# Turned attention probabilities: three PSUM banks of a unit become two, and three small transpositions become one

## The chip, the cores and the metric

The kernel runs on one core of a Trainium2 chip. The metric is the device time of one execution in microseconds (us). Five engines work side by side, each through its own list of instructions in order: PE (matrix multiplications and transpositions; its weight loads are listed as PEld), DVE (vector work), ACT (activations and copies), POOL (more vector work), SP (here it only issues DMAs). PE writes its results to PSUM, which has eight banks of 128 partitions by 512 fp32 columns; DVE and ACT read them from there.

## What is computed

Three stages follow one another: attention with a window of 128 keys and four sink keys that every query sees, then a feed-forward stage with a cosine (FFN), then a mixture of eight experts, one for each token.

```python
# B, H, S, D = 4, 8, 768, 64
keep = is_sink | in_window
scores = np.where(keep, scale * q @ k.T, -1e9)
a = np.exp(scores - scores.max(-1))
a = a / (a.sum(-1) + 1e-9)
x = (a @ v)                       # to 3072 tokens x 512
h = x @ w_in                      # 512 -> 2048
x = (h * np.cos(h)) @ w_out       # 2048 -> 512
# top-1 experts: out[e] = gate * (relu(x @ w1[e]) @ w2[e])
```

## The kernel before

The sequence of each batch is cut into two halves of 384 queries, which gives eight half-batches, hb = 0 to 7, and each half-batch into three blocks of 128 queries (t = 0, 1, 2). The eight heads are taken in four pairs (pr = 0 to 3). One pair of one half-batch is a unit; there are 32. The FFN of a half-batch runs while the units of the next half-batches run: `attn_half` and `run_ffn` are generators that hand back weights, and `merge` interleaves them by these weights, so that PE always has FFN products (tiles `hp`, L136, and `y`, L640) between the small steps of a unit. From what the generators emit, a list scheduler makes the final order of each engine's list. After it, an engine takes its instructions strictly in that order.

The change lies in `rest()` of `attn_front`, the last part of a unit. There the unnormalised probabilities `Pb` (128 queries by 272 columns: 128 older keys, 16 sinks, 128 own keys) are scaled by 1/sum (by POOL for hb = 2, by DVE from hb = 3). For a block t that is *folded*, the older and the own 128 columns were added into one square, since every query has a window over exactly one of the two at each column. Then, for each t: PE turns (transposes) the two heads' squares into a PSUM tile `pt` (L560), and DVE reads `pt` into `pT`, each square twice, once with each of two triangular masks `sides` (L148 is the helper that records it). A block that is not folded takes four transpositions or two (L569, L570) and a copy by ACT (L572). Then the 16 sink columns of both heads are copied into `pc` (L589), PE turns them, for each t by itself, into another PSUM tile `pz` (L592: 32 rows each), ACT copies `pz` to `sp` (L593), and PE multiplies `sp` and `pT` with the values, into `po`.

Units differ as follows. In hb = 0 and 1 nothing is folded. In hb = 3, 5, 7 all three blocks are, and the sinks of all three go through `pz` (12 units). In hb = 2, 4, 6 only t = 2 is folded and has sinks to be turned (12 units); t = 0 and t = 1 go through ACT. PSUM tiles of the attention part (`pq`, `pk`, `ps`, `pt`, `pz`, `po`) come from `psb`, which takes one of three banks in rotation.

Of the kernel before, what the change touches and what calls it, by code (L numbers as in the profile page):

```python
# [11 lines left out]
F32 = DT.float32  # L12
# [4 lines left out]
AF = mybir.ActivationFunctionType  # L17
# [3 lines left out]
P = 128  # L21
# [33 lines left out]
NPOOL = 3  # L55
# [6 lines left out]
def kernel(  # L62
# [23 lines left out]
    HALF = S // 2  # L86
# [227 lines left out]
    def steps(hb):  # L314
        return STEPS_0 if hb <= 1 else STEPS_1
# [80 lines left out]
    def attn_front(hb, pr):  # L396
# [138 lines left out]
        def rest():  # L535
# [16 lines left out]
            pT = apool.tile([P, 2, NQ * 256], F32, name="pT", bufs=2)  # L552
            for t in range(NQ):
                pt = psb("pt").rearrange("p (j x) -> p j x", j=2)
                first = half == 0 and t == 0
                s0 = P if first else 0
                if folded(t):
                    pt2 = pt[:, 0]
                    for j in range(2):
                        PE.transpose(pt2[:, j * P:(j + 1) * P], Pb[t][j][:, SEG:W3], ident)  # L560
                    s4 = [P, 2, 2, P]
                    tt(DVE, pT[:, :, t * 256:(t + 1) * 256].rearrange("p j (x q) -> p j x q", x=2),
                       pt2.rearrange("p (j q) -> p j q", j=2).unsqueeze(2).to_broadcast(s4),
                       sides.unsqueeze(1).to_broadcast(s4), ALU.mult)
                    yield steps(hb)[4]
                    continue
                for j in range(2):
                    if not first:
                        PE.transpose(pt[:, j, 0:P], Pb[t][j][:, 0:P], ident)  # L569
                    PE.transpose(pt[:, j, P:2 * P], Pb[t][j][:, SEG:W3], ident)  # L570
# [11 lines left out]
            t0 = 2 if half == 0 else 0  # L582
            pc = apool.tile([P, NQ, 2, NS], F32, name="pc")
            if extra:
                for t in range(t0, NQ):
                    for j in range(2):
                        POOL.tensor_copy(pc[:, t, j], Pb[t][j][:, P:SEG])
            else:
                (POOL if hb < NPOOL else DVE).tensor_copy(pc[:, t0:], Pt[:, t0:, :, P:SEG])  # L589
            pz = psb("pz")  # L590
            for t in range(t0, NQ):
                PE.transpose(pz[0:2 * NS, t * P:(t + 1) * P], pc[:, t].rearrange("p j s -> p (j s)"), ident)  # L592
            ACT.activation(out=sp[0:2 * NS, t0 * P:], in_=pz[0:2 * NS, t0 * P:HALF], func=AF.Copy)  # L593
            yield steps(hb)[5]
# [808 lines left out]
```

## Time and profile before

| | us |
|---|---|
| median of three runs | 1149.26 (1148.4 to 1151.08) |
| the profiled execution | 1149.4 |
| its span in the trace | 1147.6 |
| PE busy | 1093.7 |
| DVE / ACT busy | 716.4 / 629.4 |

The trace covers one execution; 1.8 us of its time lie around the span. In the order of time: up to 126 us the first eight units and the conversion of weights, from 126 to 690 us the 24 units of hb = 2 to 7 woven into the FFN, to 812 us the rest of the FFN, to 1090 us the experts, then the tail. The page says how long each engine was busy. A timeline row gives start, duration, engine, line, what is written from what, and in brackets how long the engine had been idle before, and which instruction released it. PE's durations overlap, since products are pipelined: the price of a PE instruction in a full stream is the distance from its start to the next start.

### The profile page before, as it was taken

Reading aid. Unit: us, or ns where it says so; the run is one execution under the profiler, and the core shown is the slowest. Engines: PE = TensorE matmul, PEld = TensorE weight load, DVE = VectorE, ACT = ScalarE, POOL = GpSimd, SP = SyncE. Lnnn points to the kernel's source line nnn. Section 1 sums busy time; section 2 is a strip of 40 time slices with the busy share of each in tenths; the row PEclk is TensorE's granted clock in tenths of the full one; section 3 lists DMA queues with packets and bytes.
Section 4 is the critical chain, followed back from the end, with each engine's and each line's share of the span. In section 5 each row is a group of like instructions: output and inputs, shape, how many; then the busy total and the mean of one; then the engine's idle time right before and its main releaser. Section 6 shows DMA issues by size and latency. Waiting matters only on the chain.

```text
span 1147.6 us, 20806 instructions
## 1 busy us (share of the span) xinstructions
PE 1093.7 (95%) x6504; PEld 936.0 (82%) x6504; DVE 716.4 (62%) x2206; ACT 629.4 (55%) x1283; POOL 224.8 (20%) x275
## 2 busy tenths in 40 slices
PE   5989999999999999999999999999999998999995
PEld 3667677888888888878888889899889997899994
DVE  6678888877876877886788774746741225622210
ACT  4878887766676676666777553434222225522221
POOL 1232224211111111111111112321112211121110
PEclk9999999999999999999999999999999999999998
DMA  6566666433333433433253223723151115111110
GB/s 149 139 193 197 195 200 168 113 86 84 95 91 83 118 82 75 112 86 83 72 118 96 69 78 107 251 62 111 47 193 53 61 39 184 33 62 41 39 42 24
DMA packets 139286, 118.56 MB, mean 103 GB/s; under 512 B 96367, under 2 KB 105583, under 8 KB 139120
## 3 DMA queue, kind: packets, MB, share of 16 engines
q1 hardware_dynamic: 134800, 103.02, 32.3%
q0 software_dynamic: 4320, 13.65, 3.6%
q8 instruction: 65, 1.06, 0.4%
q14 instruction: 101, 0.83, 0.2%
HBM read 151.06 MB, written 19.67 MB: 149 GB/s over the span
## 4 chain that ended last, share of the span: by engine, by line
PE 76%; DVE 12%; ACT 4%; DMA 4%; issue 2%; POOL 1%; SPq 0%; DVEq 0%; POOLq 0%; ACTq 0%
PE hp L136 19%; PE y L640 18%; PE m_y L136 10%; PE m_h L136 10%; PE po L136 5%; PE ps L136 4%; DMA out_dram<-m_ot,m_ids 3%; PE pl L768 1%; DVE pT L148 1%; DVE qT L148 1%; DVE ch L142 1%; DVE kl L148 1%; PE m_a L1107 1%; PE pq L445 1%; PE pt L570 1%
## 5 line engine op out<-in xcount | busy, mean ns | idle before, releaser
L148 POOL TENSOR_TENSOR g_l<-ch,g_h 128x384 fp32r<-128x384 f32 x128 | 133.4, 1043 | 552.9 <-ACT g_h L712 497.6
L136 PE MATMUL hp<-xT_h,wi_h 128*128 128x384 f32 x512 | 182.2, 356 | 2.7 <-DVE ch L148 2.7
L136 PE MATMUL hp<-xT_l,wi_h 128*128 128x384 f32 x512 | 174.7, 341 | 0.0
L136 PE MATMUL hp<-xT_h,wi_l 128*128 128x384 f32 x512 | 174.1, 340 | 0.0
L640 PE MATMUL y<-wo,g_h 128*128 128x512 f32 x384 | 157.2, 411 | 0.0
L640 PE MATMUL y<-wo_l,g_h 128*128 128x512 f32 x384 | 156.0, 406 | 0.0
L640 PE MATMUL y<-wo,g_l 128*128 128x512 f32 x384 | 154.6, 403 | 0.2 <-POOL g_l L148 0.2
L702 ACT ACTIVATE ch<-ch,cols 128x384 f32<-128x384 f32 x128 | 78.9, 617 | 119.4 <-DVE ch L145 117.6
L136 PE MATMUL m_y<-wi_h,hT 128*128 128x512 f32 x416 | 132.5, 393 | 0.7 <-ACT m_ot L1149 0.5
L145 DVE SCALAR_TENSOR_TENSOR hT<-m_h,hT 128x256 fp32r<-128x256 f32 x88 | 37.4, 425 | 151.9 <-ACTq L1301 94.9
L136 PEld LDWEIGHTS hp<-xT_h,wi_h 128*128 128x128 f32 x512 | 96.8, 189 | 10.7 <-issue 3.4
L136 PEld LDWEIGHTS hp<-xT_l,wi_h 128*128 128x128 f32 x512 | 96.9, 189 | 5.5 <-issue 1.9
L142 DVE TENSOR_SCALAR ch<-hp 128x384 int32<-128x384 f32 x128 | 71.0, 555 | 48.0 <-PE hp L136 36.2
L136 PEld LDWEIGHTS hp<-xT_h,wi_l 128*128 128x128 f32 x512 | 96.5, 189 | 1.2 <-issue 0.9
L712 ACT ACTIVATE g_h<-ch 128x384 fp32r<-128x384 f32 x128 | 66.5, 521 | 54.1 <-DVE ch L148 42.9
L148 DVE TENSOR_TENSOR ch<-ch,hp 128x384 f32<-128x384 f32 x128 | 70.4, 550 | 38.3 <-ACT ch L702 37.9
L136 PEld LDWEIGHTS m_y<-wi_h,hT 128*128 128x128 f32 x416 | 78.0, 188 | 16.9 <-issue 0.9
L532 ACT ACTIVATE Pb<-Pb,mx 128x272 f32<-128x272 f32 (+1 forms) x168 | 83.0, 496 | 9.3 <-DVE mx L516 8.4
L640 PEld LDWEIGHTS y<-wo,g_l 128*128 128x128 f32 x384 | 72.3, 188 | 14.2 <-POOL g_l L148 0.8
L1118 ACT ACTIVATE hT<-m_h 128x256 fp32r<-128x256 f32 x88 | 34.0, 387 | 88.0 <-PE m_h L136 80.9
L136 PE MATMUL m_y<-wi_l,hT 128*128 128x512 f32 x208 | 81.0, 389 | 0.0
L640 PEld LDWEIGHTS y<-wo,g_h 128*128 128x128 f32 x384 | 72.4, 189 | 10.5 <-issue 2.7
(280 smaller groups left out, 2368.1 us busy)
## 6 DMA issues: line engine op xcount, KB each, us to landing
rw<-in_moe_w_dram SPq DMA_DIRECT2D x112, 512.0 KB
wo_l<-wl_scr SPq DMA_DIRECT2D x122, 256.0 KB
cv_in<-in_moe_w_in_dram SPq DMA_DIRECT2D x16, 512.0 KB
cv_out<-in_moe_w_out_dram SPq DMA_DIRECT2D x16, 512.0 KB
y_scr<-yt SPq DMA_DIRECT2D x24, 256.5 KB
xT_h<-xg_h SPq DMA_DIRECT2D x32, 192.0 KB
xT_l<-xg_l SPq DMA_DIRECT2D x32, 192.0 KB
qn<-in_q_dram SPq DMA_DIRECT2D x56, 96.0 KB
```

The source lines that it names most:

```text
L136: PE.matmul(o, l, r, start=start, stop=stop)
L142: e.tensor_scalar(out=o, in0=i, scalar1=s1, scalar2=s2, op0=op0, op1=op1)
L145: e.scalar_tensor_tensor(out=o, in0=i0, scalar=s, in1=i1, op0=op0, op1=op1)
L148: e.tensor_tensor(out=o, in0=a, in1=b, op=op)
L445: PE.transpose(pq[:, t * P:(t + 1) * P], qn[:, t].rearrange("p j d -> p (j d)"), ident)
L532: ACT.activation(out=Pb[t][j][:, c0:c1], in_=Pb[t][j][:, c0:c1], func=AF.Exp, scale=-1.0, bias=mx[:, i:i + 1], accum_out=sm[:, i:i + 1])
L570: PE.transpose(pt[:, j, P:2 * P], Pb[t][j][:, SEG:W3], ident)
L640: i = PE.matmul(o, l, r, start=start, stop=stop)
L702: ACT.activation(out=ch, in_=ch, func=AF.Sin, scale=TWO_PI, bias=half_pi)
L712: ACT.activation(out=gh, in_=ch, func=AF.Copy)
L768: return PE.matmul(pl[0][:, 0:NE], yT[:, c, :], wg[:, c, :], start=c == 0, stop=c == KD - 1)
L1118: ACT.activation(out=hT_h[f], in_=hp, func=AF.Relu)
```

## The change

For hb = 2 to 7 (`whole`) the copy into `pc` is written ahead of the transpositions of the probabilities. The blocks t = 0 and t = 1, where folded, share one PSUM bank (columns 0 to 255 and 256 to 511). Block t = 2 takes the first half of another bank, and the sinks are turned into columns 256 to 383 of that bank, directly behind the two transpositions of t = 2, with one transposition for all blocks (96 rows for hb = 3, 5, 7; 32 rows, as before, for hb = 2, 4, 6). ACT's copy to `sp` then comes block by block: three of 32x128 in place of one of 32x384, each from another group of 32 partitions. It is written behind DVE's reading of the same bank, and both weights that the generator hands back now come together behind it. Units of hb = 0 and 1 keep their code.

```diff
--- before.py
+++ after.py
@@ -550,20 +550,38 @@
                         ts(DVE, Pb[t][j][:, c0:c1], Pb[t][j][:, c0:c1], sm[:, i:i + 1], ALU.mult)
             yield steps(hb)[3]
             pT = apool.tile([P, 2, NQ * 256], F32, name="pT", bufs=2)
+            t0 = 2 if half == 0 else 0
+            pc = apool.tile([P, NQ, 2, NS], F32, name="pc")
+            if whole:
+                (POOL if hb < NPOOL else DVE).tensor_copy(pc[:, t0:], Pt[:, t0:, :, P:SEG])
+            bank = None
             for t in range(NQ):
-                pt = psb("pt").rearrange("p (j x) -> p j x", j=2)
                 first = half == 0 and t == 0
                 s0 = P if first else 0
                 if folded(t):
-                    pt2 = pt[:, 0]
+                    if t == 2 or bank is None:
+                        bank = psb("pt")
+                        pt2 = bank[:, 0:2 * P]
+                    else:
+                        pt2 = bank[:, 2 * P:4 * P]
                     for j in range(2):
                         PE.transpose(pt2[:, j * P:(j + 1) * P], Pb[t][j][:, SEG:W3], ident)
+                    if t == NQ - 1:
+                        pz = bank[:, 2 * P:3 * P]
+                        nz = 2 * NS * (NQ - t0)
+                        PE.transpose(pz[0:nz], pc[:, t0:].rearrange("p t j s -> p (t j s)"), ident)
                     s4 = [P, 2, 2, P]
                     tt(DVE, pT[:, :, t * 256:(t + 1) * 256].rearrange("p j (x q) -> p j x q", x=2),
                        pt2.rearrange("p (j q) -> p j q", j=2).unsqueeze(2).to_broadcast(s4),
                        sides.unsqueeze(1).to_broadcast(s4), ALU.mult)
+                    if t == NQ - 1:
+                        for t_ in range(t0, NQ):
+                            z0 = 2 * NS * (t_ - t0)
+                            ACT.activation(out=sp[0:2 * NS, t_ * P:(t_ + 1) * P], in_=pz[z0:z0 + 2 * NS], func=AF.Copy)
+                        yield steps(hb)[5]
                     yield steps(hb)[4]
                     continue
+                pt = psb("pt").rearrange("p (j x) -> p j x", j=2)
                 for j in range(2):
                     if not first:
                         PE.transpose(pt[:, j, 0:P], Pb[t][j][:, 0:P], ident)
@@ -579,19 +597,19 @@
                 for t in range(NQ):
                     POOL.tensor_copy(rb[t].rearrange("p (j d) -> p j d", d=D),
                                      sm[:, 2 * t:2 * t + 2].unsqueeze(2).to_broadcast([P, 2, D]))
-            t0 = 2 if half == 0 else 0
-            pc = apool.tile([P, NQ, 2, NS], F32, name="pc")
-            if extra:
+            if not whole:
+                if extra:
+                    for t in range(t0, NQ):
+                        for j in range(2):
+                            POOL.tensor_copy(pc[:, t, j], Pb[t][j][:, P:SEG])
+                else:
+                    POOL.tensor_copy(pc[:, t0:], Pt[:, t0:, :, P:SEG])
+                pz = psb("pz")
                 for t in range(t0, NQ):
-                    for j in range(2):
-                        POOL.tensor_copy(pc[:, t, j], Pb[t][j][:, P:SEG])
-            else:
-                (POOL if hb < NPOOL else DVE).tensor_copy(pc[:, t0:], Pt[:, t0:, :, P:SEG])
-            pz = psb("pz")
-            for t in range(t0, NQ):
-                PE.transpose(pz[0:2 * NS, t * P:(t + 1) * P], pc[:, t].rearrange("p j s -> p (j s)"), ident)
-            ACT.activation(out=sp[0:2 * NS, t0 * P:], in_=pz[0:2 * NS, t0 * P:HALF], func=AF.Copy)
-            yield steps(hb)[5]
+                    PE.transpose(pz[0:2 * NS, t * P:(t + 1) * P], pc[:, t].rearrange("p j s -> p (j s)"), ident)
+                ACT.activation(out=sp[0:2 * NS, t0 * P:], in_=pz[0:2 * NS, t0 * P:HALF], func=AF.Copy)
+                yield steps(hb)[5]
+
             def band(blk):
 
                 own = blk if half == 0 else blk - 1
```

Three places show the order that the scheduler makes of it. The first is PE's list in unit hb = 3, pr = 1, from directly behind the transpositions of t = 2 past those of the sinks. `y` and `hp` are FFN products. Before:

```order
L640 MATMUL y_3139<-wo_l,g_h 128x512
L640 MATMUL y_3139<-wo_114,g_l 128x512
L640 MATMUL y_3140<-wo_114,g_h 128x512
L640 MATMUL y_3140<-wo_l,g_h 128x512
L640 MATMUL y_3140<-wo_114,g_l 128x512
L136 MATMUL hp<-xT_h,wi_h_85 128x384
L136 MATMUL hp<-xT_l,wi_h_85 128x384
L136 MATMUL hp<-xT_h,wi_l_95 128x384
L592 MATMUL pz<-ident,pc 32x128 x3
L136 MATMUL hp<-xT_h,wi_h_85 128x384
L136 MATMUL hp<-xT_l,wi_h_85 128x384
L136 MATMUL hp<-xT_h,wi_l_95 128x384
```

After, from directly behind the transpositions of t = 2 up to the first `po`:

```order
L658 MATMUL y_3132<-wo_l,g_h 128x512
L658 MATMUL y_3132<-wo_114,g_l 128x512
L572 MATMUL pt<-ident,pc 96x128
L658 MATMUL y_3133<-wo_114,g_h 128x512
L658 MATMUL y_3133<-wo_l,g_h 128x512
L658 MATMUL y_3133<-wo_114,g_l 128x512
L658 MATMUL y_3134<-wo_114,g_h 128x512
L658 MATMUL y_3134<-wo_l,g_h 128x512
L658 MATMUL y_3134<-wo_114,g_l 128x512
L136 MATMUL hp<-xT_h,wi_h_85 128x384
L136 MATMUL hp<-xT_l,wi_h_85 128x384
L136 MATMUL po<-sp_139,vs_n_137 64x384 x2
```

The turned sinks stood three `hp` and five `y` behind t = 2's transpositions, and stand two `y` behind them now; where three instructions were, there is one of 96 rows. `po`, which stood six `hp` behind the sinks, now stands six `y` and two `hp` behind them.

In the same unit, DVE's list (`kl`, `qT` belong to the next unit's keys and queries, `ch` to the FFN). Before:

```order
L148 TENSOR_TENSOR qT<-pq,qT 64x384
L148 TENSOR_TENSOR kl_2754<-pk,kT 64x4x128
L148 TENSOR_TENSOR pT<-pt,sides 128x2x256 x2
L142 TENSOR_SCALAR ch<-hp 128x384
L589 COPY pc<-Pb_3209 128x96
L145 SCALAR_TENSOR_TENSOR ch<-hp,ch 128x384
```

After:

```order
L148 TENSOR_TENSOR qT<-pq,qT 64x384
L148 TENSOR_TENSOR kl_2751<-pk,kT 64x4x128
L556 COPY pc<-Pb_3203 128x96
L148 TENSOR_TENSOR pT<-pt,sides 128x2x256 x2
L142 TENSOR_SCALAR ch<-hp 128x384
L145 SCALAR_TENSOR_TENSOR ch<-hp,ch 128x384
```

The copy into `pc` moved from behind the two `pT` readings and a step of the FFN to ahead of both, directly behind `kl`.

The last unit of hb = 3 (pr = 3), PE's list from the FFN products ahead of the sinks to the first `po` (`ps`: scores of the next unit). Before:

```order
L640 MATMUL y_3138<-wo_l,g_h 128x512
L640 MATMUL y_3138<-wo_123,g_l 128x512
L640 MATMUL y_3139<-wo_123,g_h 128x512
L640 MATMUL y_3139<-wo_l,g_h 128x512
L592 MATMUL pz<-ident,pc 32x128 x3
L640 MATMUL y_3139<-wo_123,g_l 128x512
L640 MATMUL y_3140<-wo_123,g_h 128x512
L640 MATMUL y_3140<-wo_l,g_h 128x512
L640 MATMUL y_3140<-wo_123,g_l 128x512
L136 MATMUL ps<-kT,qT 128x128
L136 MATMUL po<-sp_139,vs_n_137 64x384 x2
```

After:

```order
L136 MATMUL hp<-xT_l,wi_h_1765 128x384
L572 MATMUL pt<-ident,pc 96x128
L136 MATMUL hp<-xT_h,wi_l_1771 128x384
L136 MATMUL hp<-xT_h,wi_h_1765 128x384
L136 MATMUL hp<-xT_l,wi_h_1765 128x384
L568 MATMUL pt<-ident,Pb_3736 128x128 x2
L136 MATMUL hp<-xT_h,wi_l_1771 128x384
L136 MATMUL hp<-xT_h,wi_h_1765 128x384
L136 MATMUL hp<-xT_l,wi_h_1765 128x384
L136 MATMUL hp<-xT_h,wi_l_1771 128x384
L658 MATMUL y_3132<-wo_123,g_h 128x512
L136 MATMUL po<-sp_139,vs_n_137 64x384 x2
```

The sinks stand ahead of two transpositions of t = 1 now, which wait for the reading of t = 0 in the same bank; the rest of `y` moved behind `po`.

## Rows read from the trace of the kernel before

**Rows 1.** The page: busy us of each engine (x instructions), and its chain of waits.

```profile
...
PE 1093.7 (95%) x6504; PEld 936.0 (82%) x6504; DVE 716.4 (62%) x2206; ACT 629.4 (55%) x1283; POOL 224.8 (20%) x275
...
PE 76%; DVE 12%; ACT 4%; DMA 4%; issue 2%; POOL 1%; SPq 0%; DVEq 0%; POOLq 0%; ACTq 0%
...
```

**Rows 2.** Busy time of each engine in the window from 126 to 690 us.

```profile
...
126.00:690.00 564.00, 549.02 (x3245) 464.96 (x3245) 444.01 (x1395) 390.64 (x765) 111.15 (x125) 1.00 0.40 103
...
```

**Rows 3.** Instructions on tile pz, 126 to 690 us: min/median/max ns; then waits (us, times).

```profile
...
L592 PE MATMUL pz<-ident,pc x48: 269/272/283, 131.1 to 683.3; 128*32 128x128 f32 x48
L593 ACT ACTIVATE sp<-pz x24: 248/374/485, 131.9 to 683.6; 32x128 f32<-32x128 f32 x12, 32x384 f32<-32x384 f32 x12
...
  DVE pc L589: 1.7, 3
...
  PEld po L136: 4.6, 15
...
```

**Rows 4.** Instructions on tile pt, the same window, columns as in Rows 3.

```profile
...
L148 DVE TENSOR_TENSOR pT<-pt,sides x48: 665/684/694, 130.6 to 682.2; 128x512 f32<-128x512 f32 x48
...
```

**Rows 5.** Timeline, PE, one unit: start us, us, instruction [idle before <-releaser].

```profile
...
248.84 0.41 PE L560 MATMUL pt<-ident,Pb 128*128 128x128 f32 x2 [0.47 <-DVE pT L148]
...
251.08 0.38 PE L560 MATMUL pt<-ident,Pb 128*128 128x128 f32 x2
...
251.53 0.40 PE L640 MATMUL y<-wo,g_l 128*128 128x512 f32 x1
...
251.76 0.40 PE L640 MATMUL y<-wo,g_h 128*128 128x512 f32 x1
...
252.63 0.34 PE L136 MATMUL hp<-xT_l,wi_h 128*128 128x384 f32 x1
...
252.80 0.34 PE L136 MATMUL hp<-xT_h,wi_l 128*128 128x384 f32 x1
...
252.98 0.49 PE L592 MATMUL pz<-ident,pc 128*32 128x128 f32 x3
...
253.48 0.34 PE L136 MATMUL hp<-xT_l,wi_h 128*128 128x384 f32 x1
...
254.47 0.87 PE L136 MATMUL po<-sp,vs_n 128*64 128x384 f32 x4
...
```

**Rows 6.** Timeline of the same unit, DVE and ACT.

```profile
...
250.18 0.69 DVE L148 TENSOR_TENSOR kl<-pk,kT 64x512 fp32r<-64x512 f32 x1
...
250.91 1.29 DVE L148 TENSOR_TENSOR pT<-pt,sides 128x512 f32<-128x512 f32 x2
...
252.57 0.20 DVE L589 COPY pc<-Pb 128x96 f32<-128x96 f32 x1
...
253.29 0.62 ACT L702 ACTIVATE ch<-ch,cols 128x384 f32<-128x384 f32 x1 [3.09 <-DVE ch L145]
...
253.93 0.48 ACT L593 ACTIVATE sp<-pz 32x384 f32<-32x384 f32 x1
...
```

**Rows 7.** Timeline of a second unit, PE and DVE, DVE late.

```profile
...
298.14 0.41 PE L560 MATMUL pt<-ident,Pb 128*128 128x128 f32 x2 [0.41 <-DVE qT L148]
...
302.09 1.89 DVE L148 TENSOR_TENSOR pT<-pt,sides 128x512 f32<-128x512 f32 x3
...
304.36 0.20 DVE L589 COPY pc<-Pb 128x96 f32<-128x96 f32 x1
...
304.71 0.49 PE L592 MATMUL pz<-ident,pc 128*32 128x128 f32 x3 [0.61 <-DVE pc L589]
...
306.25 0.87 PE L136 MATMUL po<-sp,vs_n 128*64 128x384 f32 x4
...
```

**Rows 8.** Timeline of a third unit, DVE and PE.

```profile
...
343.39 0.69 DVE L759 COPY yT<-yT 128x512 f32<-128x512 f32 x1
...
344.57 0.56 DVE L148 TENSOR_TENSOR kl<-pk,kT 64x384 fp32r<-64x384 f32 x1
...
344.93 0.38 PE L560 MATMUL pt<-ident,Pb 128*128 128x128 f32 x2
...
```

## The prediction

> **What bounds the kernel now.** I read the page first: PE is busy 95% of the span and holds 76% of the chain of waits, DVE 12% [rows 1]. An average hides stages, so next the window in which all changed units lie, 126 to 690 us: PE is busy 549.02 of 564.00 us, DVE 444 and ACT 391 [rows 2]. PE is the bound there too, and only 15 us of idle time are left in it. So time comes from there in two ways alone: PE does less, or PE waits less. A step of another engine counts by the wait that it makes on PE. Then the views of the two tiles: the sinks' transpositions, their copy, and who waits for them [rows 3], and the reading of the turned probabilities [rows 4]. At last I went through the timeline of units, to see what PE does between the steps and what DVE and ACT do meanwhile [rows 5 to 8].
>
> **What the change removes.** In 12 units three sink transpositions become one: of the 48 in the window [rows 3] 24 remain. The 269 to 283 ns of such a row overlap their neighbours, so the price is the distance between starts. From the `hp` product at 252.80 to the one at 253.48 there are three transpositions and one further product; two product steps of 0.17 (252.63 to 252.80) are 0.34, and 0.34 of the 0.68 remain for three, 0.113 each [rows 5]. Nothing in the trace has 96 rows: if such a one costs as much as three of 32, nothing is saved, if as one, 24 are. I take one: t = 2's pair of 128 rows at 251.08 and one `y` of 0.23 take 0.45 up to the `y` at 251.53, so 0.11 each [rows 5], the same as those of 32. So PE loses 24 x 0.113 = 2.7 us of work. That is 0.23 in each of the 12 units. It is certain as work, and all of it lies on PE.
>
> **What it adds on ACT.** For 12 units one copy of 32x384, 485 ns, becomes three of 32x128, 248 ns each [rows 3]: 0.74 in place of 0.48, 0.26 more, or 3 us over all 12. ACT has 173 us idle in the window [rows 2], so this costs nothing by itself; it counts where `po` waits for the last copy.
>
> **What it makes wait.** The sinks had a bank of their own. Now the built order has three links in a row that were apart: the sinks' transposition waits for `pc`; DVE's reading of t = 2 waits for that transposition; ACT's first copy waits for DVE's reading, though it reads other columns of the bank. One reading is 0.68 us [rows 4]. Behind a waiting transposition stands all of PE's list, FFN products included; behind the waiting copies stands ACT's FFN work. The Trainium skill, "PSUM — Partial Sum Buffer", section "PSUM bank collisions raise a hardware error", says that two engines must not touch the same bank in the same quadrant of partitions at once, reads with reads included, so that software must order them. By it the third link is needed wherever banks are shared, and speaks against this change: without it the copy would start 0.68 earlier than I reckon below. The trace of before has no such pair, so no row shows it.
>
> Three units show what the links cost.
>
> *First unit* (hb = 3, pr = 1) [rows 5, 6]. The second block's transpositions start at 248.84 in both orders, held by the reading of the first. From there PE has six `hp` (to 250.14), one `y`, t = 2's two (t = 2 was held by nothing that is longer now), and two `y` of 0.23 (251.53 to 251.76), and comes to the sinks at 251.05. DVE ends `kl` at 250.87 and then copies `pc`, 0.20, to 251.07; with 0.15 from a copy's end to the transposition's start (304.56 to 304.71 in [rows 7]) that gives 251.25: a wait of 0.2 that was not there, since before `pc` had ended at 252.77 for a transposition at 252.98. Then one transposition, six `y`, two `hp`: `po` is reached at about 253.1. DVE reads both blocks from 251.07 to 252.43; three copies take ACT to 253.2 (it was idle until 253.29), and `po` starts at about 253.25, with a wait of 0.15. Before, `po` waited 0.1 for the copy that ended at 254.41. New waits 0.2 + 0.15 - 0.1 = 0.25, saved 0.23: nothing gained. The other units of this kind vary around it, by my reckoning from 0.05 to 0.25 of new waits, as `kl` ends a little earlier or later. I take 0.2 for ten units (nine with pr = 0 to 2, and the last unit of hb = 7, in another order): +2.0.
>
> *Second unit* (hb = 3, pr = 3; hb = 5 has the same order) [rows 7]. DVE is late: it comes to the readings at 302.09 only. Before, PE waited at the sinks to 304.71, where the last product before them allowed about 303.92: 0.8 (the row books 0.61 of it). Now `pc` goes first, to 302.29, and PE is at the sinks at 301.3 (from 298.14: two transpositions, nine `y`, five `hp`), so it waits 1.15, to 302.44. Then, with three `hp`, two transpositions, four `hp` and one `y`, `po` is reached at 304.2, where the readings (to 304.33) and three copies (303.7 to 304.45) let it start at 304.5: 0.3. That is 1.45 for 0.8: +0.65 in each of two units, +1.3.
>
> *Third unit* (hb = 4, pr = 1; hb = 6 likewise) [rows 8]. Here the number of transpositions stays, but the order moves: five `y` come between the first block and the second instead of three, so the second now comes to DVE's `yT` copy, which ends at 344.08, and the third to `kl`, which ends at 345.13 (before it started at 344.93). Each waits 0.15: +0.3, twice +0.6.
>
> *The other ten units* (four of hb = 2, whose `pc` POOL makes, and three each of hb = 4 and 6) keep one sink transposition and lose no work; their new waits lie behind other waits or FFN products as far as I can follow them: 0, with -0.2 and +0.3 for each from the units above as bounds, hence -2 to +3.
>
> **Sum.** -2.7 + 2.0 + 1.3 + 0.6 = +1.2 us. Part of any shift, up or down, is given back: PE's next wait for DVE, ACT or a DMA absorbs it, and 15 us of such waits are there [rows 2]; I take half of it away, +0.6. The profiled execution took 1149.4 (1147.6 of it span), 0.14 above the median of 1149.26. 1149.4 + 0.6 = 1150.0. About 0.2%, 2.3 us, is what a measurement of this kernel can tell from no change: this is none, 1147.0 to 1151.6.
>
> **Rivals.** *The waits do not come about.* If `kl` and `pc` end some tenths earlier, as they may when DVE's list shifts with PE, the sinks find `pc` ready and `po` finds the copies done. For it: the waits in the first unit are 0.2 and 0.15 on a reckoning of events some 4 us long. Besides, the three waits of PE for `pc`, 1.7 us, and the waits of `po` for the copy, 4.6 us in 15 cases [rows 3], are there to be lost. Then all of the 2.7 is kept and about half of the 1.7: 1149.4 - 2.7 - 0.8 = 1145.9. Against it: DVE reaches `pc` behind `kl` in every unit I followed. Chance 0.24 for a gain over 0.2%, mostly between 1145 and 1147.
>
> *The chain gets longer and `po` waits for it: slower.* Place: from `pc` through the transposition, the reading and the copies to `po`. Price: in the first unit it leaves `po` about 0.15 late; each further 0.1 us by which DVE is late goes into PE's wait one for one. If DVE is half a microsecond later than I reckon in each of the 12 units with three copies (the second unit shows that it can be over one), that is 6.0 on top of the +1.2; with half absorbed as above, +3.6: 1153.0. This decides from about 0.3 us in each: 12 x 0.3 + 1.2 = 4.8, half of it 2.4. For it: DVE is 79% busy in the window. Against it: half the sites have FFN products to spare. Chance 0.30.
>
> *It does not do what it says.* The shared bank is meant to free one in the rotation. But the second block waits for the reading of the first already before [rows 5], so the two had one bank by the rotation; nothing new comes free at once. This is in the forecast and gives its number.
>
> **How the numbers follow.** Forecast (no difference that can be told) 0.46, faster 0.24, slower 0.30. The range leaves out the ends of both: 1146.3 to 1153.8. Faster means under 1147.0, slower over 1151.6.
>
> **What would show it.** Right: PE instructions fewer by 24; 24 rows of sink transpositions in it in place of 48; a new wait of PE on `pc` in units of hb = 3 and 5, some 3 us in all against 1.7; ACT's copies start when a reading ends; the window's PE busy time lower by 2 to 3 us with its length within 2. Wrong, fast side: PE's idle time in the window stays at 15 us or falls, and the 2.7 appears whole. Wrong, slow side: PE's waits for `pc` and `sp` in this window together are over 10 us, against 6.3 (1.7 + 4.6).

## The result, and the profile after

The change makes the kernel slower: 1158.45 us (1157.57 to 1159.33) against 1149.98 (1148.4 to 1151.08), a ratio of 1.0072 with a 95% interval of 1.0057 to 1.0087. Measured once more beside other kernels it was 1158.11 against 1151.42, 1.0054 (1.0035 to 1.0074). The forecast was 1150.0 and no difference, with a range up to 1153.8.

The page of the changed kernel, its busy times and its chain of waits, which answer to [rows 1]:

```profile
PE 1098.0 (95%) x6480; PEld 938.4 (81%) x6480; DVE 719.9 (62%) x2206; ACT 631.9 (55%) x1307; POOL 224.6 (19%) x275
...
PE 73%; DVE 14%; DMA 4%; ACT 4%; issue 2%; POOL 1%; SPq 0%; ACTq 0%; DVEq 0%; POOLq 0%
```

PE issues the 24 instructions fewer that were foreseen (6480 for 6504), yet its busy time rose by 4.3 us, and in the chain PE's share fell from 76 to 73% while DVE's rose from 12 to 14%. A record of PE is drawn out where the granted clock is lower: a `y` product takes 0.63 us in a stretch at 0.50 that is shown below, 0.40 in [rows 5]. So a busy time that rises need not mean more work. The stretch of [rows 2], six us longer now:

```profile
126.00:696.00 570.00, 551.14 (x3221) 465.13 (x3220) 447.65 (x1396) 393.88 (x791) 112.19 (x125) 0.99 0.39 102
```

PE has 18.9 us without a record in it, against 15 before, and its granted clock (the third number from the end) is 0.99 in place of 1.00. PE's busy time in it is 2.1 us higher, where the prediction had 2 to 3 us less.

To see where the time went I laid the two traces on one another by the transpositions of the queries (`pq`), one group for each unit, and by the first transposition of the experts (`m_a`). The last part of a unit, where the change lies, runs behind the `pq` of the unit that follows it. The rows in the kernel before (start, duration, instruction), where the first eight units are done, where those of hb = 2 are done, and at the experts:

```profile
123.26 0.49 PE L445 MATMUL pq<-ident,qn 128*128 128x128 f32 x3
...
218.65 0.49 PE L445 MATMUL pq<-ident,qn 128*128 128x128 f32 x3
...
841.01 1.03 PE L1107 MATMUL m_a<-ident,m_yg 128*128 128x128 f32 x8
```

The same three in the changed kernel:

```profile
123.82 0.49 PE L445 MATMUL pq<-ident,qn 128*128 128x128 f32 x3
...
222.73 0.49 PE L445 MATMUL pq<-ident,qn 128*128 128x128 f32 x3
...
847.86 1.03 PE L1125 MATMUL m_a<-ident,m_yg 128*128 128x128 f32 x8
```

They are 0.56, 4.08 and 6.85 us late. Read as differences of such starts for every unit, the time was lost like this (a unit's step is the growth of the lateness over its last part; the second measurement's trace is beside it):

| lost in, us | hb = 2 | hb = 3 | hb = 4 | hb = 5 | hb = 6 | hb = 7 to the experts | sum |
|---|---|---|---|---|---|---|---|
| changed kernel | 3.51 | 0.56 | 0.51 | 0.58 | 0.52 | 0.60 | 6.28 |
| the same, second trace | 3.11 | 0.59 | 0.53 | 0.58 | 0.51 | 0.63 | 5.95 |

From hb = 3 on the two traces agree within 0.05 us per half-batch. Of the 9.2 us between the two spans (1156.8 and 1147.6), 0.56 lie ahead of this stretch and 2.35 behind the start of the experts, where the code is the same; these were not followed up, and no part of what follows rests on them. Two traces of one and the same kernel differ there too, by up to 2 us ahead and 0.8 behind. In the tables below "sum" is always the stretch from the end of the first eight units to the experts.

### The profile page after: what moved, and what is told of

It is laid out like the page before. It is cut to its first block, busy times and chain, and to the rows that moved or that the text cites. A ratio compares the mean times of both kernels' runs of the same rounds, so it can differ in the third digit from the quotient of the medians.

```text
span 1156.8 us, 20792 instructions
## 1 busy us (share of the span) xinstructions
PE 1098.0 (95%) x6480; PEld 938.4 (81%) x6480; DVE 719.9 (62%) x2206; ACT 631.9 (55%) x1307; POOL 224.6 (19%) x275
## 4 chain that ended last, share of the span: by engine, by line
PE 73%; DVE 14%; DMA 4%; ACT 4%; issue 2%; POOL 1%; SPq 0%; ACTq 0%; DVEq 0%; POOLq 0%
PE hp L136 18%; PE y L658 17%; PE m_h L136 10%; PE m_y L136 10%; PE po L136 5%; PE ps L136 5%; DMA out_dram<-m_ot,m_ids 3%; DVE pT L148 2%; DVE qT L148 2%; DVE kl L148 2%; PE pl L786 1%; DMA cv_in<-in_moe_w_in_dram 1%; PE pt L588 1%; PE pq L445 1%; PE m_a L1125 1%
```

## Where the waits are

The copies to `sp` in the changed kernel, their min/median/max and waits, which answer to [rows 3]:

```profile
L580 ACT ACTIVATE sp<-pt x48: 249/267/269, 132.0 to 690.5; 32x128 f32<-32x128 f32 x48
...
  DVE pT L148: 32.2, 17
...
  PEld po L136: 7.4, 16
```

Before, `po`'s weight load waited 4.6 us for the copy; now 7.4, and ACT stands idle for 32.2 us in all ahead of the copies until DVE has read, where before it stood 12.0 us until the sinks were turned. Idle time of ACT is no loss by itself; `po`'s wait is. The first unit of the prediction (hb = 3, pr = 1), PE, DVE, POOL and ACT, which answers to [rows 5, 6]:

```profile
253.04 0.41 PE L568 MATMUL pt<-ident,Pb 128*128 128x128 f32 x2 [0.45 <-DVE pT L148]
...
254.39 0.69 DVE L148 TENSOR_TENSOR kl<-pk,kT 64x512 fp32r<-64x512 f32 x1
...
254.48 1.00 POOL L148 TENSOR_TENSOR g_l<-ch,g_h 128x384 fp32r<-128x384 f32 x1 [4.70 <-ACT g_h L730]
...
255.11 0.44 DVE L556 COPY pc<-Pb 128x96 f32<-128x96 f32 x1
255.59 1.29 DVE L148 TENSOR_TENSOR pT<-pt,sides 128x512 f32<-128x512 f32 x2
...
255.61 0.31 PE L572 MATMUL pt<-ident,pc 128*96 128x128 f32 x1 [0.18 <-DVE pc L556]
...
256.91 0.83 ACT L580 ACTIVATE sp<-pt 32x128 f32<-32x128 f32 x3 [2.50 <-DVE pT L148]
...
257.32 0.33 PE L136 MATMUL hp<-xT_l,wi_h 128*128 128x384 f32 x1
...
257.79 0.87 PE L136 MATMUL po<-sp,vs_n 128*64 128x384 f32 x4
```

The links are the ones foreseen, in their order: `kl` ends at 255.08, `pc` follows, PE stands at the sinks from about 255.27 to 255.61, DVE reads both blocks from 255.59, three copies run from 256.91, and `po`, which could start at 257.49, starts at 257.79. But the copy into `pc` takes 0.44 us, not the 0.20 of [rows 6]: it starts while POOL's `g_l` runs (254.48 to 255.48) and ends 0.07 us behind it, where before POOL was idle.

Half-batch 2 holds more than half of the loss. The place where most of it arises, POOL, DVE and PE in its third unit, after:

```profile
175.39 0.22 DVE L539 RECIPROCAL sm<-sm 128x2 f32<-128x2 f32 x2
...
175.57 1.29 POOL L148 TENSOR_TENSOR g_l<-ch,g_h 128x384 fp32r<-128x384 f32 x1 [4.66 <-ACT g_h L730]
...
176.84 2.81 POOL L142 TENSOR_SCALAR Pb<-Pb,sm 128x128 f32<-128x128 f32 x6
...
177.70 0.68 PE L588 MATMUL pt<-ident,Pb 128*128 128x128 f32 x2 [1.72 <-POOL Pb L142]
```

And before:

```profile
172.35 0.22 DVE L539 RECIPROCAL sm<-sm 128x2 f32<-128x2 f32 x2
...
172.60 3.31 POOL L142 TENSOR_SCALAR Pb<-Pb,sm 128x128 f32<-128x128 f32 x6 [4.89 <-DVE sm L539]
...
173.63 0.38 PE L570 MATMUL pt<-ident,Pb 128*128 128x128 f32 x2
```

DVE comes to the reciprocal of the sums (L539) at 175.39, behind four conversions of weights (`cv_a`, `wo_l`) and a step of the FFN that stood behind it before; it was there at 172.35, and only 0.6 of this is lateness that the unit had from its start (171.46 for 170.88). In POOL's list `g_l` went ahead of the scaling as well. POOL therefore scales the probabilities from 176.84 on, not from 172.60, and PE, whose next transposition needs them, waits 1.72 us. The unit's order of work is another one, though hb = 2 saves no transposition.

## Experiments

### In which half-batches the time is lost

Theory A: the loss sits in hb = 2, whose lists the scheduler ordered anew; the links of the shared bank cost a little elsewhere. Rival B: the links cost alike in all 24 units. Three kernels (e1 to e3) take the changed code for some half-batches and keep the code of before for the others (first branch: the changed code, second: that of before; "hb > 2" in the first kernel, "hb == 2" in the second, "half == 1" in the third):

```diff
+            if not whole or hb > 2:
+                ...
+            else:
+                ...
```

e1, from hb = 3 on: 

> Half-batch 2 keeps the code of before; the changed code runs from hb = 3 on. Theory A (half-batch 2 lost most: its lists were ordered anew, PE waited 1.2 and 1.7 us there and ran at a granted clock of 0.62 to 0.85 afterwards, +3.9 us by the alignment of the two traces at 218.65 and 222.73, less what stood before): about 1152 to 1154, and the granted clock is 1.00 from 126 to 224 us. Rival B (the links between pc, the transposition, the reading and the copies cost in every unit alike, 8.5 us over 24): 1157, since 20 of the 24 units keep them.

e2, hb = 2 alone: 

> The changed code in half-batch 2 alone, before elsewhere; no transposition is saved there. Theory A: 1150 + 3.9 = about 1154, with the granted clock under 1.00 between 140 and 182 us. Rival B: 4 of 24 units, 1.4 us: about 1151.4.

e3, hb = 3, 5, 7 alone: 

> The changed code for hb = 3, 5, 7 alone, where 24 transpositions go; 2, 4 and 6 as before. Theory A, with the sum of the prediction for these 12 units (-2.7 + 2.0 + 1.3): within 1 us of before, 1149 to 1151.5. Rival B: half of 8.5, 1154. If the links cost nothing: 1147.3.

e5, the changed kernel once more: 

> The changed kernel as it is, beside the others. The change in half-batch 2 alone cost 3.2 us at the medians and the change from hb = 3 on cost 0.3, which adds up to 1.003 of before, not to 1.0072. If the two add up: 1154 to 1155. If they work on each other (the bank rotation of every later unit shifts with the banks that hb = 2 takes): 1157 to 1159 again, with steps of 0.15, 0.3 and 0.05 us in the units of hb = 4 and 6, which are missing where hb = 2 keeps its code.

| changed code in | ratio (95%) | hb = 2 | hb = 3 | hb = 4 | hb = 5 | hb = 6 | sum, us |
|---|---|---|---|---|---|---|---|
| all | 1.0054 (1.0035 to 1.0074) | 3.11 | 0.59 | 0.53 | 0.58 | 0.51 | 5.95 |
| hb = 3 on | 1.0000 (0.9987 to 1.0014) | -0.29 | 0.69 | -0.11 | 0.67 | -0.12 | 1.00 |
| hb = 2 | 1.0025 (1.0012 to 1.0037) | 2.44 | 0.11 | 0.27 | 0.13 | 0.24 | 2.83 |
| hb = 3, 5, 7 | 1.0014 (1.0004 to 1.0025) | -0.32 | 0.67 | 0.54 | 0.09 | 0.43 | 1.91 |

Half-batch 2 is the greatest part, as theory A had it; that every unit pays alike (B) has fallen. With the old code in hb = 2 the rest of the change comes to no measurable difference, so A's number for it (1152 to 1154) was too high; that for hb = 3, 5, 7 (1149 to 1151.5) was too low for the 1152.9 us measured. One thing moves all numbers of hb = 2 a little: the nine traces in which DVE's list there is that of before come to -0.46 to -0.08 against this one trace of before, so the losses of hb = 2 are rather some tenths larger than written. The parts do not add up, however: 2.83 and 1.00 are not 5.95. What the second kernel shows in hb = 4 and 6, whose code is that of before in it, tells why: their second units lose 0.32 us each, the same as in the changed kernel (0.31), and lose nothing (0.00) where hb = 4 and 6 have the changed code and hb = 2 the old one. So this loss isn't made by the code of these units. In PE's list of such a unit five `y` stand between the first block and the second, as in the changed kernel. What is handed on from unit to unit is the count of banks taken from the rotation of three. Up to these two units a kernel of this document has taken fewer banks than the kernel before by a multiple of three (0, or 9 and 21 in the first kernel here), or by another number (4, 8, 13, 16, 25), counted from its code. In the five traces with a multiple of three the step of both units is between -0.02 and 0.01, in the ten others 0.23 to 0.41. So the count goes with the loss wherever it was measured; a kernel that changes the count and nothing else was not run.

### The waits in hb = 2, and the clock

The same two windows of hb = 2 in three traces (busy us of PE, PEld, DVE, ACT and POOL with counts, then the granted clock, the share of the DMA engines and GB/s). The changed kernel:

```profile
141.00:150.00 9.00, 8.17 (x32) 5.91 (x33) 9.00 (x23) 7.25 (x14) 3.02 (x4) 0.81 0.83 251
173.00:183.00 10.00, 8.10 (x34) 6.29 (x34) 7.00 (x20) 7.00 (x15) 4.62 (x9) 0.83 0.67 196
```

The changed kernel, second trace:

```profile
141.00:150.00 9.00, 8.17 (x41) 6.39 (x40) 9.00 (x25) 7.21 (x12) 3.02 (x5) 1.00 0.85 259
173.00:183.00 10.00, 7.92 (x35) 6.07 (x34) 6.60 (x19) 6.92 (x15) 5.01 (x9) 0.83 0.69 196
```

The changed code in hb = 2 alone:

```profile
141.00:150.00 9.00, 8.16 (x41) 6.39 (x40) 9.00 (x25) 7.16 (x12) 3.02 (x5) 1.00 0.81 252
173.00:183.00 10.00, 7.74 (x39) 5.49 (x37) 7.04 (x21) 6.87 (x15) 5.25 (x9) 1.00 0.67 201
```

The waits of PE are in all three (0.83 or 0.84 us at the first place, 1.72, 2.06 and 2.04 us at the second), the drop of the clock in both windows, in one, and in none; the expectation for the third, a clock under 1.00, did not come true. In the first trace PE had waited 0.83 us for DVE at 144.07 and 1.72 at 177.70. The stretch behind the first of them is granted 0.50 of full speed, the lower of the two levels, 1.2 GHz instead of 2.4:

```profile
145.00:148.00 3.00, 3.00 (x8) 2.32 (x8) 3.00 (x9) 2.61 (x5) 0.00 (x0) 0.50 0.81 218
```

```profile
144.07 0.72 PE L136 MATMUL ps<-kT,qT 64*128 64x272 f32 x2 [0.83 <-DVE mx L516]
...
146.51 0.63 PE L658 MATMUL y<-wo,g_l 128*128 128x512 f32 x1
146.93 0.63 PE L658 MATMUL y<-wo,g_h 128*128 128x512 f32 x1
```

The `y` products there start 0.42 us apart in place of 0.23. Over hb = 2 the lists of PE, DVE, ACT and POOL are the same in all three. The losses of hb = 2, 3.51, 3.11 and 2.44, then say what is whose, as far as three traces can: about 2.4 us are waits and the order, and the slower clock behind the waits adds some 0.4 at the first place and 0.7 at the second, in some executions and not in others.

### Shared bank or place in the code

Theory A splits here: it is the place in the code that costs (A1), or the shared bank (A2). In e6 the sinks get a bank of their own again, with everything else as changed:

```diff
-                        pz = bank[:, 2 * P:3 * P]
+                        pz = psb("pz")[:, 0:P]
```

> The changed kernel, but the sinks are turned into a bank of their own; the order in the code and everything else stays. DVE then need not wait for the sinks' transposition, nor ACT for DVE's reading. Theory A1, the place in the code (directly behind t = 2, pc ahead) reorders half-batch 2 and costs there: +3 remain in hb = 2, while the units of hb = 3, 5, 7 lose their wait of po: 0.3 less in each, 1153 to 1155 in all. Theory A2, the shared bank is what costs, in hb = 2 too: back to 1150 or less.

In e7 ACT's copies come ahead of DVE's reading in the shared bank (the loop of the copies moved up, behind the sinks' transposition):

```diff
                         PE.transpose(pz[0:nz], ...)
+                        for t_ in range(t0, NQ):
+                            ...
                     tt(DVE, pT[...
-                        for t_ in range(t0, NQ):
-                            ...
```

> The changed kernel, but in the shared bank ACT copies the sinks before DVE reads t = 2, not after. If the link from DVE's reading to ACT's copies makes po late: about 0.3 us less in each of 12 units, 3 us less than the changed kernel, though DVE's reading now waits for three copies, 0.74. If po's lateness only moves from sp to pT: no difference.

In e8 banks are shared and there is one transposition, but `pc`, the sinks and both weights at the places of before stand:

```diff
-            pz = psb("pz")
-            for t in range(t0, NQ):
-                PE.transpose(pz[0:2 * NS, t * P:(t + 1) * P], pc[:, t]..., ident)
+            pz = bank[:, 2 * P:3 * P] if whole else psb("pz")
+            if whole and half == 1:
+                PE.transpose(pz[0:2 * NS * NQ, 0:P], pc..., ident)
+                ...
```

> Banks shared as in the changed kernel, and one transposition of 96 rows, but the sinks are turned where they were before: behind DVE's reading of t = 2 and behind the handing back of its weight, with the pc copy there too. Theory A1 (the place in the code costs): half-batch 2 keeps its order of before, no step there, and the whole is near the kernel with the merged transposition alone, 1147 to 1149. Theory A2 (the shared bank costs): 1152 or more, with steps in every unit.

| kernel | ratio (95%) | hb = 2 | hb = 3 | hb = 4 | hb = 5 | hb = 6 | sum, us |
|---|---|---|---|---|---|---|---|
| own bank | 1.0031 (1.0016 to 1.0045) | 3.23 | -0.08 | 0.16 | 0.07 | 0.35 | 3.72 |
| copies first | 1.0024 (1.0011 to 1.0038) | 1.22 | 0.19 | 0.61 | 0.23 | 0.61 | 2.49 |
| late sinks | 0.9982 (0.9968 to 0.9997) | -0.08 | 0.60 | -1.24 | 0.61 | -1.25 | -0.77 |

With a bank of their own the loss of hb = 2 stays whole and that of hb = 3 and 5 goes, about 0.6 us for each of the two half-batches: the shared bank is the cost there, and in hb = 2 it is not: the order in the code is. The waits of the copies and of `po` in the kernel with the own bank show it:

```profile
  PE pz L572: 21.6, 14
...
  PEld po L136: 1.7, 5
```

The copies wait for PE again and not for DVE; `po` waits 1.7 us in place of 7.4. Copying first came to at least the 3 us less that were expected, but in another way: of the 3.5 us between 5.95 and 2.49 hb = 2 gives 1.9 (1.22 in place of 3.11), hb = 3 and 5 only 0.4 each, and the stretch from hb = 7 to the experts 1.0. The second units of hb = 3 and 5 lose 0.10 instead of 0.31, but the last ones lose 0.31 and 0.33 that they did not lose before: there DVE's reading, free at 304.10, starts at 304.64, behind the three copies. In the third unit of hb = 2 the wait of 1.72 us is gone, though the two weights still come together:

```profile
172.76 0.22 DVE L539 RECIPROCAL sm<-sm 128x2 f32<-128x2 f32 x2
```

Late sinks clear hb = 2, and hb = 3 and 5 keep their 0.6: both with the theory. The -1.2 of hb = 4 and 6 was not expected and is taken up below.

Two more kernels tell which of the three things that "late sinks" puts back frees hb = 2. In e13 the weight of t = 2 is handed back ahead of the copies, not behind them together with that of the sinks:

```diff
                     if t == NQ - 1:
+                        yield steps(hb)[4]
                         for t_ in range(t0, NQ):
                             ...
                         yield steps(hb)[5]
-                    yield steps(hb)[4]
+                    else:
+                        yield steps(hb)[4]
```

> The changed kernel, with one line moved: the weight of t = 2 is handed back before ACT's copies, that of the sinks behind them, in place of both behind them. If the joined weights reordered half-batch 2: its loss of 3.1 to 3.5 us goes, the steps from hb = 3 on stay as in the changed kernel (+2.8 up to the experts), so about 3.3 less than the changed kernel, 1154 to 1155. If the place of the sinks or the early copy reordered it: 1158, as the changed kernel.

In e14 the sinks are turned only behind that weight as well, in the shared bank, and the early `pc` copy stays:

> The changed kernel, with the weight of t = 2 handed back behind DVE's reading and the sinks turned behind that, in the same bank; the early pc copy stays. Half-batch 2: no loss, as in e8. From hb = 3 on: if turning the sinks directly behind t = 2 is what costs there, the steps of 0.3 in the second units of hb = 3, 5, 7 fall to 0.1 or less, 1150 to 1152; if the shared bank costs (the reading, then the transposition, then the copies in a row), they stay or grow.

e13 came to 1.0020 (1.0005 to 1.0035), 1152.68 us where 1154 to 1155 were expected: hb = 2 loses 1.35 instead of 3.1 to 3.5, and every unit from hb = 3 on keeps the changed kernel's step within 0.03 us. The 1.72 us of waiting in the third unit are gone. The window of this place, and one behind another wait, in the fourth unit:

```profile
173.00:183.00 10.00, 10.00 (x63) 8.15 (x62) 9.98 (x21) 7.22 (x15) 3.27 (x6) 1.00 0.78 242
...
200.00:205.00 5.00, 5.00 (x27) 4.02 (x28) 4.94 (x8) 2.64 (x7) 3.59 (x4) 0.66 0.32 105
```

So the joined weights are needed for the greater part of the loss of hb = 2. They do not make it alone: with the copies ahead of the reading the weights are joined, too, and that wait is gone as well. Either edit gives DVE another list than the changed kernel's. The rest is new: the wait moved to the fourth unit, where PE stood 0.62 us for DVE's `qT` and 0.65 for its `ch`, and the clock fell behind it. With the sinks turned behind the weight as well, hb = 2 loses nothing (-0.15), and the ratio is 1.0020 (1.0006 to 1.0034), hb = 3 and 5 now losing 0.78 and 0.77. The early `pc` copy is not what costs in hb = 2. One thing parts the traces that lose in hb = 2 from the others: in the six that lose (1.22 to 3.51) DVE's list there is another one than before, in the nine that lose nothing (-0.46 to -0.08) it is the same, instruction by instruction.

### What the saved transpositions are worth

e4 is the kernel before with the merged transposition alone (bank, place and the other transpositions as before):

```diff
-            for t in range(t0, NQ):
-                PE.transpose(pz[0:2 * NS, t * P:(t + 1) * P], pc[:, t]..., ident)
-            ACT.activation(out=sp[0:2 * NS, t0 * P:], in_=pz[0:2 * NS, t0 * P:HALF], func=AF.Copy)
+            if whole and half == 1:
+                PE.transpose(pz[0:2 * NS * NQ, 0:P], pc..., ident)
+                for t in range(NQ):
+                    ACT.activation(out=sp[0:2 * NS, t * P:(t + 1) * P], in_=pz[t * 2 * NS:(t + 1) * 2 * NS, 0:P], func=AF.Copy)
+            else:
+                ...
```

> Kernel before, with one edit: for hb = 3, 5, 7 the three transpositions of the sinks are one of 96 rows and the copy to sp is three of 32x128; the bank, the place of the pc copy and the banks of the probabilities stay. If one transposition of 96 rows costs as one of 32 and the copies are hidden: -2.7, 1147.3. If po waits 0.26 more for three copies in each of 12 units: -2.7 + 3.1, 1150.4. If 96 rows cost like three times 32: 1150 or more.

e9, the same again: 

> The kernel before with the merged transposition alone, a second time, beside the others of this call. It was at 0.9966 of before. If that was its own: 0.995 to 0.998 again, with the step of -1.3 us in the first units of hb = 4 and hb = 6. If it was the spread of executions: 0.999 to 1.001.

e11, the kernel before with the early `pc` copy alone (the copy moved ahead of the loop of the transpositions, for hb = 2 on):

> The kernel before, with the copy into pc ahead of the transpositions of the probabilities and nothing else. If the copy is slowed by POOL's work there: its rows show 0.44 us in place of 0.20 in units pr = 1 and 2 of hb = 3, 5, 7, without a wait of PE, since the sinks' transposition comes late: 0.999 to 1.001, and less wait of pz for pc in the units pr = 3 (0.6 each), so up to 1.8 us faster. Half-batch 2: no step if the early copy is not what reorders it.

e12, both: 

> Merged transposition and early copy together, all banks and the place of the transposition as before. If both gains hold: 0.994 to 0.997, better than either. If the scheduler's order shifts so that hb = 4 and 6 lose their step of -1.3: 0.999.

e10, merged, and the first two blocks in one bank:

> The merged transposition, and on top the first two blocks in one bank; the sinks keep a bank of their own, and their place. Tells the first sharing from the second. The two blocks had one bank by the rotation already where the second waits for the reading of the first, so nothing is lost there: as the merged one, 0.996 to 0.998. If the sharing shifts the rotation and later units lose by it: steps of 0.1 to 0.3 in the units of hb = 4 and 6.

| kernel | ratio (95%) | hb = 2 | hb = 3 | hb = 4 | hb = 5 | hb = 6 | sum, us |
|---|---|---|---|---|---|---|---|
| merged | 0.9966 (0.9953 to 0.9980) | -0.34 | 0.25 | -1.33 | 0.26 | -1.34 | -2.19 |
| merged, again | 0.9971 (0.9961 to 0.9981) | -0.41 | 0.25 | -1.32 | 0.26 | -1.34 | -2.25 |
| early `pc` | 1.0013 (1.0004 to 1.0022) | -0.46 | 0.35 | 0.14 | 0.36 | 0.14 | 0.21 |
| both | 0.9990 (0.9978 to 1.0003) | -0.31 | -0.03 | 0.10 | -0.08 | 0.10 | -0.89 |
| merged, first two share | 1.0004 (0.9993 to 1.0015) | -0.38 | 0.47 | 0.26 | 0.64 | -0.89 | 0.27 |

The merged transposition alone beats both kernels: 1146.85 and 1147.41 us at the medians, 0.3% under the kernel before in both measurements. But its gain isn't where the work was saved. In hb = 3 and 5 it loses a quarter of a us. The unit that the prediction worked out first, in this kernel:

```profile
253.01 0.27 PE L592 MATMUL pz<-ident,pc 128*96 128x128 f32 x1
...
253.32 0.55 ACT L594 ACTIVATE sp<-pz 32x128 f32<-32x128 f32 x2 [3.08 <-PE pz L592]
...
254.39 0.27 ACT L594 ACTIVATE sp<-pz 32x128 f32<-32x128 f32 x1
...
254.72 0.87 PE L136 MATMUL po<-sp,vs_n 128*64 128x384 f32 x4 [0.20 <-ACT sp L594]
```

The sinks' single transposition is there, and of the three copies the scheduler sets an FFN step of ACT between the second and the third; `po` starts at 254.72 and has waited 0.20 for the third copy, in the kernel before it started at 254.47. What is gained comes in the first unit of hb = 4, 1.33 us, and of hb = 6. There the kernel before waits twice with its transpositions:

```profile
322.18 0.44 PE L560 MATMUL pt<-ident,Pb 128*128 128x128 f32 x2 [0.56 <-ACT pT L572]
...
325.04 0.33 PE L569 MATMUL pt<-ident,Pb 128*128 128x128 f32 x1 [0.57 <-DVE kl L148]
```

and the merged one turns the same blocks earlier, in another order and without a wait:

```profile
321.16 0.27 PE L569 MATMUL pt<-ident,Pb 128*128 128x128 f32 x1
...
321.59 0.38 PE L560 MATMUL pt<-ident,Pb 128*128 128x128 f32 x2
```

This is the list scheduler's doing: code of these units was not touched. So the gain is luck, as far as the merging goes, and small edits take it away: with the early copy on top it is gone (0.14 in place of -1.33), and with the first two blocks in one bank, which was expected to keep it, it is gone in hb = 4 and stays in hb = 6 (-0.04 and -1.44 in their first units).

"Early `pc`" and "both" differ by the merging alone, and their steps in units with pr = 1 and 2 of hb = 3 and 5 are 0.10 and -0.11 against -0.08 and -0.31 (0.11 and -0.11 against -0.09 and -0.31): 0.18 to 0.20 us per unit is what two transpositions less are worth where nothing waits. In pr = 0 and 3 the steps of the two kernels are equal: there `po` waits for the copies, of which the merged kernel has three, 0.83 us together, where the other has one of 0.48. Who waited for them, early `pc` alone, then both:

```profile
  PEld po L136: 2.4, 8
```

```profile
  PEld po L136: 5.6, 14
```

So the price was about right, and only half of the units can cash it in. Rows of the two kernels for the first unit, early `pc` alone:

```profile
249.73 1.02 POOL L148 TENSOR_TENSOR g_l<-ch,g_h 128x384 fp32r<-128x384 f32 x1 [4.71 <-ACT g_h L714]
...
250.35 0.46 DVE L556 COPY pc<-Pb 128x96 f32<-128x96 f32 x1
```

and both:

```profile
250.54 1.02 POOL L148 TENSOR_TENSOR g_l<-ch,g_h 128x384 fp32r<-128x384 f32 x1 [4.71 <-ACT g_h L719]
...
251.17 0.46 DVE L556 COPY pc<-Pb 128x96 f32<-128x96 f32 x1
```

The copy takes 0.46 us in both and ends 0.06 us behind POOL's `g_l`, at the same place in DVE's list as in the changed kernel. The slow copy costs little there (the steps of the units with pr = 1 and 2 are -0.31 to 0.11), and with a bank of their own for the sinks the same units of hb = 3 lose 0.17 and -0.04 in place of 0.31 and 0.10: most of its cost comes by the links of the shared bank. Early `pc` alone was expected at 0.999 to 1.001 or faster, by waits saved in pr = 3; those units lose 0.36 and 0.38 instead.

## Why the prediction was wrong, step by step

- **PE as the bound, and 24 transpositions less.** Right: the counts fell by 24. *The price*, 0.113 for one, 0.23 for a unit: 0.18 to 0.20 were measured. *Its reach* was wrong. The sum took 2.7 us for 12 units; where it could be isolated it came to 1.1 us (0.21 and -0.89 as sums), since in pr = 0 and 3 `po` waits for three copies in place of one.
- **First unit.** New waits of 0.25 were reckoned, +0.02 net (251.07 and 0.15 are 251.22, not 251.25; nothing hangs on it); the unit loses 0.31. The links stood as foreseen, but `pc` took 0.44 where 0.20 was put in, which moves the transposition and, through the reading, `po`: 0.34 and 0.30 of waiting in place of 0.20 and 0.15; the three copies took 0.83 together, not 0.74. The price of `pc` came from a place where POOL was idle; the order put it where POOL works, in the units with pr = 1 and 2. These lose 0.3 and 0.1, those with pr = 0 0.14. Over hb = 3, 5 and 7 the loss is about 1.7 us where the sum had 0.6 (-2.7 + 2.0 + 1.3).
- **Second unit.** +0.42 net was reckoned; 0.01 and 0.03 were measured (hb = 3 and 5). Its rows:

```profile
306.50 0.20 DVE L556 COPY pc<-Pb 128x96 f32<-128x96 f32 x1
...
306.75 0.31 PE L572 MATMUL pt<-ident,pc 128*96 128x128 f32 x1 [0.62 <-DVE pc L556]
```

  PE waited 0.8 us at the sinks (from about 305.95, by the products from 303.60 on), as long as before, not 1.15: the unit starts 4.6 us later than before, but `pc` only 4.4, and the gap behind the copy is 0.05, not 0.15. `po` waited the 0.3 foreseen.
- **Third unit.** +0.3 was reckoned for hb = 4 and 6, 0.31 was measured in each. The two waits stand where they were foreseen, behind `yT` (it ends at 348.88, the transposition starts at 348.93) and behind `kl` (349.93 and 349.99). The mechanism was incomplete all the same: the code of these units alone does not make the order (0.00 with hb = 2 unchanged), and old code in them has it, too (0.32 with hb = 2 changed).
- **The other ten units: the step that failed.** The four of hb = 2 were put down at 0, with +0.3 each as a bound. They lost 3.1 to 3.5 us, more than half of the 6.0 to 6.3 lost in all; the other six lost about 0.2 in each half-batch. The prediction looked there for links of the shared bank, of which hb = 2 has few, and did not read what the joined weights, with the copies behind the reading, do to the list of DVE: conversions went ahead of the reciprocals that POOL, and then PE, wait for. The clock behind the waits was not in the reckoning at all. The order of DVE's list, which was at hand without any time, would have shown it.
- **Half of a shift is given back.** Not so: from hb = 3 to the experts every step stays, and the lateness at the experts is the sum of them. The idle time of PE did not take the loss up.
- **The rule on a shared bank** (the Trainium skill, "PSUM — Partial Sum Buffer", section "PSUM bank collisions raise a hardware error": two engines on one bank and quadrant of partitions have to be put in order by software). The runs agree as far as they go: with the order `po` waits 7.4 us for ACT's copies, which stand behind DVE's reading, and with a bank of their own 1.7 us, and hb = 3 and 5 lose nothing. What would happen without the order wasn't tried.
- **The rival "slower"** named the chain from `pc` to `po`, which is there and costs 1.7 us in hb = 3, 5 and 7. It did not name hb = 2, and its condition, 0.3 us in each of the 12 units with three copies, did not come about on the average (0.14). That the time came out on its side is luck. The sign it gave, more than 10 us of waits for `pc` and `sp` together, holds: 5.5 (weight loads) and 2.3 (products) for `pc`, 7.4 and 1.2 for `sp`.

What stays open: whether the count of banks in the rotation alone makes the 0.3 us in hb = 4 and 6, why the medians of the changed kernel lose 8.5 and 6.7 us where its aligned traces lose 6.28 and 5.95, and why the merged kernel's medians gain more (2.8 and 4.1 us) than its aligned traces (2.2).

## What to carry to other kernels

An edit that moves where a generator hands back its weights can change a list scheduler's order far from the steps that it is about; compare the lists of every engine over the whole stretch, first of all where a third kind of work is woven in, before working out the edited steps. Merge small transpositions if they can keep their bank and their place: the saving was 0.1 us for each here, and only where PE is not about to wait. A copy that moves must be priced at the place where it goes, with what the other engines do there.

## What was not expected of the hardware

A copy of 128x96 by DVE took 0.20 us where POOL was idle and 0.44 to 0.46 us where it started while a POOL product (`g_l`) ran; each of these ended 0.06 to 0.07 us behind the end of the product. In the changed kernel all six copies of this size at such a place took 0.44 or 0.45, and none of the others of this size over 0.21. And waits of PE of 0.8 to 2.1 us (in one kernel two of 0.6) were followed, in some executions and not in others, by some 3 us at a granted clock of 0.50, which is 1.2 GHz; the same places, with a wait as long, also ran on at 1.00.
